# Summing the last five tiles of x in fp32 on TensorE, and turning h in one product, at the start of a two-stage attention and GEGLU kernel

## Chip, cores, metric

One core of one Trainium2 chip. The metric is the device time of one execution in microseconds; several executions of each kernel are timed. The profiled execution gives a trace and a span, from the first to the last instruction, that is some 1.7 to 2.1 us shorter than the device time.

## The reference

```python
# x: (4, 12416, 128) fp32; inducing: (32, 128); d_ff = 1536
def mab(q, kv):                                   # attention, scale = 1/sqrt(128)
    a = softmax(scale * q @ kv.T); return a @ kv
h   = mab(inducing, x)                            # 32 rows for each batch
y   = mab(x, h)                                   # one row for each token
g   = y @ w_gate
ffn = (gelu(g) * (y @ w_val)) @ w_out             # gelu with erf
out = y + sigmoid(y @ w_res) * ffn
```

The kernel folds the last four lines: `y` is `softmax * h`, so `h @ w_gate`, `h @ w_val` and `h @ w_res` are computed once for each batch (called `hgv` and `hra` below), and the softmax weights (`rt`) are multiplied with those.

## The kernel before

The first batch has a prologue of its own; after it, a long planned loop runs all gelus of all batches, with the next batch's attention in the background. The prologue has three stages. (1) Each of 13 tiles of x (97 blocks of 128 rows, 8 to a tile) is split into fp16 `hi` and `lo`, `hi` is turned on PE, scores and exps `e` follow, and `e` times (`lo` with a column of ones, `hi`) is summed in PSUM; the sum is copied out as `nacc`. (2) `finish_h` adds four strips and divides; `turn_h` turns h. (3) The second softmax, the first layer's three slices (`hgv`), the residual's product (`hra`), the load of the gelu's table, the first gelu.

```python
def accumulate(b, j0, j1, first, last):           # cut
    for j in range(j0, j1):
        o = acc[cq * M:(cq + 1) * M, :]           # one of four strips of 32 rows
        pe.matmul(o[:, 0:P + 1], e, lo_t[b, k][:, jj, :P + 1], ...)
        pe.matmul(o[:, 0:P], e, hi_t[b, k][:, jj, :], ...)
    if last: ve.tensor_copy(nacc_t[b], acc[:, :P + 1])

def first_layer(b, c):
    bank = bank_g()                               # a PSUM bank of its own
    for r, w in ((slice(0, 64), wG), (slice(64, 128), wV)):
        pe.matmul(bank[r, :], ht_t[b][:, r], w[:, c:c + TOK], start=True, stop=True)
    ve.tensor_scalar(hgv_t[b][:, c:c + TOK], bank, parts, None, op0=AL.mult)

for n in range(ntile + 2):                        # stage 1
    hi_next(n + 1)
    if n < ntile:       convert_lo(0, tiles[n], ve); turn_pe(0, tiles[n])
    if 1 <= n <= ntile: exps("a", 0, n0, n0 + w, bank_v())
    if n >= 2:          accumulate(0, n0, n0 + w, n == 2, n == ntile + 1)
for i in range(2):    weight_cast(i, act)
for i in range(2, 5): weight_cast(i, po)
finish_h(0); turn_h(0)                            # stage 2
...                                               # stage 3: exps, sums, slices
first_layer(0, 2 * TOK)
res_layer(0, ve)
gel = konst.tile([P, 1], FP32, name="gel")
act.activation(gel, parts, AC.Gelu, bias=0.0, scale=1.0)   # loads the table
warm = bank_f()
for i in range(3):
    pe.matmul(warm, wG[:, :P], wG[:, :TOK], start=True, stop=True)
```

The softmax here doesn't subtract the row's maximum and nothing guards it: scores larger than these inputs give would overflow.

## Time and profile before

| | kernel before |
|---|---|
| time, median of 3 runs (range) | 772.82 us (771.55 to 773.31) |
| span of the profiled run | 770.5 us |
| `nacc` read out of PSUM | 26.90 us |
| scores of the second softmax begin (H) | 29.10 us |
| first gelu | 35.51 us |
| from the first gelu to the end | 735.0 us |

ScalarE (ACT) runs nearly without a break from the first gelu to the end, so an edit of the prologue is worth what it moves the first gelu by. Lines from the order of time: start us, length us, engine, line, operation, out<-in; in brackets the idle time before it and what ended it.

```profile
24.35 1.83 POOL L488 CAST wG<-ge 128x1024 bf16<-128x1024 f32 x1 [22.53 <-DMA ge<-in_moe_w_gate_dram]
25.58 0.36 PE L162 MATMUL v<-I1T,xt 128*128 128x32 f16 x8 [0.48 <-ACT xt L141]
34.09 0.31 PE L249 MATMUL g<-wR,ht 128*64 128x128 bf16 x1
```

The first is a weight cast on GpSimd (POOL), the second are the scores of the last tile of x, the third is the residual's product.

### The profile page before, as it was taken

The page shows a single profiled execution, that of the slowest core. Times are in us where ns is not written, and L with a number is a line of the kernel's source. Part 1 is how long each engine was busy: PE and PEld are TensorE (multiplying, and loading weights), DVE is VectorE, ACT ScalarE, POOL GpSimd, SP SyncE. Part 2 cuts the span into 40 slices and gives each one's busy share as a digit, 9 for nine tenths or more (in the row PEclk, how much of TensorE's full clock was granted, in tenths as well). Part 3 has the DMA queues.
Part 4 walks back from the last instruction along what each step waited for, and adds up shares of the span by engine and source line. Part 5 has one row for each costly group of instructions (what it writes and reads, how often), then busy time and mean ns, then how long its engine had stood idle before and what let it go on. Part 6 is the DMA issues. An engine that isn't in the chain of part 4 may idle for free.

```text
span 770.5 us, 23888 instructions
## 1 busy us (share of the span) xinstructions
PE 738.9 (96%) x9583; PEld 432.5 (56%) x9583; DVE 741.2 (96%) x735; ACT 753.3 (98%) x1506; POOL 467.4 (61%) x470
## 2 busy tenths in 40 slices
PE   6799999999999999999999999999999999999997
PEld 4455555565655655565655555556565555555555
DVE  7699999999999999989999999998999999999997
ACT  6899999999999999999999999999999999999997
POOL 0526988822787978923377797961367773443334
PEclk9889999999999999999999999999999999999999
DMA  8314589701055677521035496750105431110101
GB/s 340 124 45 129 134 191 188 165 30 43 31 119 110 157 176 192 141 46 43 29 65 112 112 210 154 139 150 29 39 21 128 87 88 43 42 43 29 42 30 60
DMA packets 118448, 78.15 MB, mean 101 GB/s; under 512 B 96672, under 2 KB 99392, under 8 KB 118336
## 3 DMA queue, kind: packets, MB, share of 16 engines
q1 hardware_dynamic: 118336, 76.62, 39.2%
q8 instruction: 75, 1.23, 0.7%
q14 instruction: 37, 0.30, 0.1%
HBM read 27.87 MB, written 25.43 MB: 69 GB/s over the span
## 4 chain that ended last, share of the span: by engine, by line
PE 47%; ACT 35%; issue 10%; DVE 4%; POOL 3%; DMA 1%; SPq 0%; ACTq 0%; DVEq 0%; POOLq 0%
ACT ge L368 23%; PE f L391 22%; PE g L357 12%; PE v L357 7%; PE g L399 3%; DVE u L362 3%; ACT at L410 3%; ACT th L405 3%; ACT e L166 2%; ACT fe L419 2%; ACT xt L141 1%; POOL lo L124 1%; ACT L166 1%; DMA xf<-in_x_dram 1%; DMA ge<-in_x_dram 1%
## 5 line engine op out<-in xcount | busy, mean ns | idle before, releaser
L362 DVE TENSOR_TENSOR u<-ge,v 128x1024 bf16<-128x1024 f32 x584 | 671.7, 1212 | 8.2 <-PE g L357 1.9
L368 ACT ACTIVATE ge<-g 128x512 f32<-128x512 f32 x1164 | 608.3, 661 | 2.7 <-PE g L357 1.6
L391 PEld LDWEIGHTS <-u 128*128 128x128 bf16 x4656 | 270.8, 98 | 206.3 <-issue 200.4
L391 PE MATMUL f<-wO,u 128*128 128x128 bf16 x4656 | 374.4, 221 | 4.0 <-DVE th L423 0.5
L357 PE MATMUL g<-rt,hgv 32*128 32x512 f16 x1152 | 337.7, 380 | 7.3 <-ACT ge L368 0.4
L357 PE MATMUL v<-rt,hgv 32*128 32x512 f16 x1152 | 222.3, 385 | 2.5 <-DVE u L362 1.5
L424 POOL TENSOR_TENSOR at<-at,th 128x512 f32<-128x512 f32 (+1 forms) x99 | 123.6, 1248 | 147.8 <-DVE th L423 66.1
L357 PEld LDWEIGHTS <-hgv 32*128 32x128 bf16 x2400 | 75.3, 91 | 87.8 <-issue 22.8
L420 POOL TENSOR_TENSOR th<-th,fe 128x512 f32<-128x512 f32 (+1 forms) x35 | 42.2, 1205 | 92.9 <-ACT fe L419 92.9
L294 POOL TENSOR_TENSOR a<-e,z 128x1024 f16<-128x1024 f32 (+1 forms) x48 | 89.8, 1880 | 5.7 <-DMA hgv<-a 5.4
L124 POOL TENSOR_TENSOR lo<-xf,hi 128x1024 f16<-128x1024 f32 x36 | 76.8, 2135 | 0.2
L399 PE MATMUL g<-hra,rt 128*128 128x128 f16 x768 | 72.1, 219 | 1.5
L410 ACT ACTIVATE at<-g 128x512 f32<-128x512 f32 (+1 forms) x100 | 65.0, 651 | 0.0
L405 ACT ACTIVATE th<-g 128x512 f32<-128x512 f32 (+1 forms) x100 | 64.3, 650 | 0.3 <-PE g L399 0.3
L399 PEld LDWEIGHTS <-rt 128*128 128x128 f16 x768 | 50.8, 98 | 12.4 <-issue 10.4
L423 DVE SCALAR_TENSOR_TENSOR th<-th,f 128x512 f32<-128x512 f32 (+1 forms) x65 | 44.1, 678 | 3.0 <-PE f L391 0.6
L118 POOL CAST hi<-xf 128x1024 f16<-128x1024 f32 x36 | 37.4, 1038 | 11.1 <-DMA xf<-in_x_dram 6.7
L421 POOL TENSOR_TENSOR at<-at,fe 128x512 f32<-128x512 f32 (+1 forms) x35 | 42.1, 1204 | 0.0
L162 PEld LDWEIGHTS <-xt 128*128 128x128 f16 x768 | 23.4, 97 | 7.2 <-issue 3.0
L166 ACT ACTIVATE e<-g 128x512 f32<-128x512 f32 (+3 forms) x40 | 20.4, 600 | 2.4 <-PE g L162 2.2
L419 ACT ACTIVATE fe<-f 128x512 f32<-128x512 f32 (+1 forms) x35 | 22.8, 650 | 0.0
L273 POOL TENSOR_TENSOR a<-a 128x256 f32<-128x256 f32 (+8 forms) x48 | 20.0, 416 | 3.8
(113 smaller groups left out, 261.0 us busy)
## 6 DMA issues: line engine op xcount, KB each, us to landing
out_dram<-at SPq DMA_DIRECT2D x96, 256.0 KB, 2.2
xf<-in_x_dram SPq DMA_DIRECT2D x38, 512.0 KB, 4.5
ge<-in_x_dram SPq DMA_DIRECT2D x10, 512.0 KB, 8.2
rt<-a SPq DMA_TRANSPOSE x48, 3.1
xt<-hi SPq DMA_TRANSPOSE x36, 4.2
ge<-in_moe_w_gate_dram SPq DMA_DIRECT2D x1, 512.0 KB, 9.3
ge<-in_moe_w_val_dram SPq DMA_DIRECT2D x1, 512.0 KB, 9.5
ge<-in_moe_w_out_dram SPq DMA_DIRECT2D x1, 512.0 KB, 4.9
```

Source lines behind the costliest of these rows:

```text
L124: eng.tensor_tensor(lo[:, :w, :P], xf_t.pop((b, k))[:, :w, :], hi_t[b, k][:, :w, :], AL.subtract)
L166: act.activation(e[:, (j0 - t0) * M:(j1 - t0) * M], bank[:, :(j1 - j0) * M], AC.Exp, bias=0.0, scale=scale)
L294: eng.tensor_tensor(a2[:, :n], ev[:, o:o + n, :].unsqueeze(2).to_broadcast([P, n, Q, M]), z[:, o:o + n].unsqueeze(2).unsqueeze(3).to_broad ...
L357: pe.matmul(*t[n], start=True, stop=True)
L362: ve.tensor_tensor(u[:, :n], ge_t.pop(value)[:, :n], v_t.pop(value)[:, :n], AL.mult)
L368: act.activation(ge_t[i][:, h * TOK:h * TOK + n], gb[:, :n], AC.Gelu, bias=0.0, scale=1.0)
L391: pe.matmul(self.ffn[:, k, :], u_t[self.gi, si][:, o:o + P], wO[:, fc, :], start=first, stop=not self.todo, skip_group_check=True)
L399: pe.matmul(bank[:, k * P:(k + 1) * P], rt_t[self.b, self.k][:, self.j0 + k, :], hra_t[self.b][:, s, :], start=True, stop=True)
L405: act.activation(self.th[:, :self.tw], self.mix(0), AC.Tanh, bias=0.0, scale=0.5)
L410: act.activation(self.at[:, :self.tw], self.mix(1), AC.Copy, bias=0.0, scale=1.0)
L423: ve.scalar_tensor_tensor(th, th, 1.0, f, AL.add, AL.mult)
L424: (ve if self.gi == ngrp - 1 else po).tensor_tensor(at, at, th, AL.add)
```

## The change

The intent: relieve VectorE (DVE) and ScalarE in stage 1, which both are full from 15 to 25 us, by summing the five tiles that land last in fp32, as they were loaded, on PE; their exps are added up first, so that four one-column products give the denominators. Then turn and divide h in one product; load the weights behind x; and reorder stage 3, so that ScalarE's exps come first.

```diff
+            if b == 0 and k in whole:
+                pe.matmul(o[:, 0:P], e, xf_t[b, k][:, jj, :], start=False, ...)   # fp32
+                continue
+    def sum_whole(n0, w, last):          # s = sum of the exps of the fp32 tiles, on DVE
+        for s in (e_of.pop("s"), e):
+            for q in range(0, w, Q):
+                pe.matmul(acc_t[0][:, P:P + 1], s[:, q * M:(q + Q) * M], one, ...)
+    def turn_first_h(b):
+        pe.matmul(tp[:, 0:M], na[:, P:P + 1].to_broadcast([P, P]), strips[:, 0, :], ...)
+        pe.matmul(tp[:, P:2 * P], na[:, 0:P], row, ...)
+        ve.reciprocal(zi, tp[:, 0:M])
+        ve.tensor_tensor(ht, tp[:, P:2 * P], zi, AL.mult)       # cut
-            convert_lo(0, tiles[n], ve)
-            turn_pe(0, tiles[n])
+            if tiles[n] not in whole:
+                convert_lo(0, tiles[n], ve)
+            turn_pe(0, tiles[n], ve if n in (9, 11, 12) else act)
+    whole = tuple(tiles[n] for n in (8, 9, 10, 11, 12))
+    for i in range(2):                   # two empty buffers ahead of the weights
+        p_ge.tile([P, 2 * TOK], FP32, name="ge", tag="ge")
-    finish_h(0)
-    turn_h(0)
+    turn_first_h(0)
 ... exps of the second softmax ahead of the slices
-    first_layer(0, 0)
+    layers = bank_v()                                   # one tile of two PSUM banks
+    first_layer(0, 0, layers[:, :TOK])
+    first_layer(0, TOK, layers[:, TOK:])
+    finish_h(0)
+    layers = bank_v()
+    first_layer(0, 2 * TOK, layers[:, :TOK])
+    res_layer(0, ve, layers[:, TOK:])                   # the other half of the same tile
-    warm = bank_f()
-    for i in range(3):
+    warm = bank_g()
+    for i in range(2):
```

## The prediction

> **What bounds the kernel now.** I read the page's busy shares first, then the chain of waits, then the first 40 us in order of time, because the diff touches only the first batch's prologue.
>
> ```profile
> PE 738.9 (96%) x9583; PEld 432.5 (56%) x9583; DVE 741.2 (96%) x735; ACT 753.3 (98%) x1506; POOL 467.4 (61%) x470
> ```
>
> ScalarE is busy 98% of the span: from the first gelu on, the program is a loop that ACT fills. The change leaves that loop's plan as it is, so its worth is how far it moves the start of the first gelu. The timeline gives that start, and the steps on the way to it:
>
> ```profile
> 24.49 1.03 ACT L141 ACTIVATE xt<-g 128x1024 f16<-128x1024 f16 x1
> 25.98 0.38 ACT L166 ACTIVATE e<-v 128x256 f16<-128x256 f32 x1 [0.18 <-PE v L162]
> 26.90 0.29 DVE L187 COPY nacc<-f 128x129 f32<-128x129 f32 x1 [1.62 <-PE f L182]
> 27.25 0.49 PE L195 MATMUL g<-nacc,strips 128*128 128x129 f32 x2 [0.42 <-DVE nacc L187]
> 28.39 0.33 PE L214 MATMUL g<-ident,nacc 128*128 128x128 f32 x1 [0.65 <-DVE nacc L200]
> 29.10 0.55 PE L162 MATMUL g<-ht,xt 128*128 128x32 f16 x16 [0.38 <-DVE ht L216]
> 33.76 1.28 ACT L542 ACT_TABLE_LOAD   x1
> 35.09 0.38 PE L357 MATMUL g<-rt,hgv 32*128 32x512 f16 x1
> 35.51 0.60 ACT L368 ACTIVATE ge<-g 128x512 f32<-128x512 f32 x1 [0.25 <-PE g L357]
> ```
>
> Three stretches follow: up to 26.90 the sums over x; 26.90 to 29.10 (2.20 us) the turning of h; 29.10 to 35.51 (6.41 us) the second softmax's start, the folded weights and the table load. The view by windows says who bounds the first one:
>
> ```profile
> 15.00:20.00 5.00, 4.20 (x108) 3.20 (x106) 5.00 (x6) 5.00 (x10) 0.00 (x0) 1.00 1.03 410
> 20.00:25.00 5.00, 4.20 (x120) 3.25 (x118) 5.00 (x6) 5.00 (x9) 0.65 (x1) 1.00 0.79 283
> 25.00:30.00 5.00, 2.95 (x72) 1.85 (x65) 1.39 (x5) 2.77 (x7) 3.50 (x7) 1.00 0.40 116
> ```
>
> The columns after the length are PE, weight load, DVE, ACT, POOL, granted clock, DMA share, GB/s. From 15 to 25 us DVE and ACT are both full; PE has 16% left. The DMA is full to about 22 us too: the last tile of x, issued near 10.1 us, is 11.6 us under way and lands near 21.7.
>
> **What the skill says.** (1) The Trainium skill, "FP8 and Floating Point Precision", TensorE Precision Notes: a true fp32 product takes four passes. The trace agrees in kind: one fp32 product of 129 columns (L195) stands as two loads and two matmuls, some 0.11 us apart, so about 0.22 us, where an fp16 one takes 0.055. (2) "TensorEngine Tiling (Array Packing)", Available Configurations and Key Properties: 128x32 tiles give four independent column tiles, and changing the tiling mode drains the engine. The trace agrees for fp16: the last tile's 16 accumulating matmuls start at 26.41 and the engine that waits for them goes on at 26.90, where 16 in a row would need 0.9 us. No fp32 ones are packed before. (3) "VectorE: DVE Perf Modes", the perf-mode tier table: fp32 tensor_tensor runs at one element a cycle, tensor_copy up to twice that. Here `lo` takes 1.22 us and `hi` 0.69 for 1024 elements, and the fp16 copy out of PSUM 0.425 for 512. (4) "TensorE: Matmul & The Clock Gate", Part 1: a gate halves the clock after a quiet free-running window of 3.4 us. The trace shows 0.50 from about 30.9 to 34.3 and 37.7 to 44.5 us: one and two such windows.
>
> **Part 1, five tiles in fp32.** DVE loses five `lo` (5 x 1.14 = 5.7 us, start to start) and gains two `hi` (2 x 0.60), three copies out of PSUM (3 x 0.60, from 0.425 for half the size) and three sums (256 fp32 elements, 0.42, or 0.34 apart): 4.0. So DVE is relieved by 1.7 us. ACT loses two `hi` and three `xt` (5 x 0.94 = 4.7). PE pays: per tile, 16 packed fp16 matmuls (0.34) become 8 packed fp32 ones. If the four strips stay concurrent, a strip has 2 matmuls x 2 passes x 0.107 = 0.43; with loads and drain I take 0.55. New on PE are also four one-column products with `s` as weights: they pay the loads, 2 x 0.11 each, 0.88 in all, just before the last accumulation.
>
> I laid the three engines' orders (the built program gives order and waits) side by side with these durations. From the last unchanged point (14.85) DVE runs hi7, lo6, hi8, lo7, hi9 to 18.9, hi10 to 19.75, copies n9, hi11 to 20.95, then waits for the last tile (21.7). PE becomes the bound there: a round is transposes 0.49, scores 0.28, accumulation 0.55, together 1.32. Its fp32 accumulations start at 20.86, 22.19, 23.46, 24.44; the one-column products run 24.99 to 25.87; the last accumulation 25.87 to 26.42, plus 0.23 to its reader: 26.65. The same table for the kernel before gives 27.19 where 26.90 was measured, so I take off 0.29: **nacc at 26.36, 0.54 us earlier**. Each 0.15 us more per accumulation costs 0.75 in all (five tiles).
>
> **Part 2, h in one product.** Before: copy, product (0.49), reciprocal, scaling, transpose, copy, 2.20 us. After: copy 0.29; two fp32 products, 0.49 + 0.22; a reciprocal of 32 columns, 0.36 (28 took 0.33), which in the built program waits for both products; one multiply 0.29; five hand-overs of 0.05. Sum 1.84, **0.36 earlier**. Scores of the second softmax thus begin at 28.2 (H).
>
> **Part 3, from H to the first gelu.** ACT has less idle: its exps now end near H+4.0, table and `gel` near H+5.5 (6.15 before). But the order of the waits is new. PE issues, in this order: third slice of first_layer, res_layer, two warm-up matmuls, first gate. In the built program res_layer's load waits for DVE's third `hgv`, because both use halves of one PSUM tile, and the second slice waits for the first `hgv` in the same way. DVE's chain: `a` ends H+1.88, `rt` H+3.0, hgv 0.65, wait for the slice 0.46, hgv 0.65, reciprocal 0.2, hf 0.36, hgv 0.72: H+6.05. Then res_layer 0.1, two warm-ups 0.43, gate 0.38 and hand-overs: first gelu near **H+7.1 at full clock, H+8.0 at half**, against H+6.41. So ACT, done earlier, waits over a microsecond for PE, and this stretch gives back 0.7 to 1.5, say 1.0.
>
> **Part 4, weights.** The two empty tiles only swap which buffers the two pieces of w_out take: the first now waits until POOL has cast w_gate (26.2 in place of 22.4) and lands near 31. Its cast follows POOL's sums, near 33; the first use is after 37. Hidden. The other pieces are issued within 0.6 us of where they were.
>
> **Sum.** -0.54 - 0.36 + 1.0 = +0.1 us: three terms that nearly cancel. After the first gelu ACT goes on as before; it idled about 1.0 us between 39 and 45 us because of the half clock, and what falls in there can move half a microsecond either way. I go 0.5 below the sum, because the hand-overs are counted in full in part 3 and some will overlap: **772.4 us**.
>
> **Rivals.** *A: packed fp32 does not pack as well.* In-order pairs of passes on one strip could hold up the next strip: about 1.0 per accumulation, nacc at 28.4, loop 2 us later, 774.8. With no concurrency at all (8 x 0.22 + drain, 1.9) nacc is at 32.9 and the time 779. For it: no packed fp32 is in the trace. Against: the fp16 pairs before use one strip for `lo` and `hi` in the very same order, and overlapped. 20% for the first, 4% for the second. *B: the PSUM wait in part 3 does not bite*, and the loop starts when ACT is ready (H+5.9): 1.4 us gained, 771.4, or 770.5 if the clock windows help too. For it: ACT's relief is real, and the order looks meant for it. Against: the waits are in the program. 25%. *C: only the clock windows matter.* They are free-running, so the half-speed stretches fall elsewhere in each run; three runs before span 1.8 us, more than every term here. Then it is 772.8 give or take 0.9. *D: x lands late and hides everything*: the last tile at 21.7 would bound DVE; but then PE, not DVE, has the later work, so it changes little.
>
> **Range and chances.** The terms' spread is about 1 us either way, the slow fp32 adds a tail upward of 2, B one downward of 2: 770.2 to 775.0 holds 8 in 10. Faster by over 2% would need 15 us, twice what the loads and sums could free; slower by over 2% needs unpacked fp32 and more.
>
> **What would show it.** Right: the five fp32 groups about 0.55 us long each, PE over 90% busy from 20 to 26 us, nacc near 26.4; from nacc to the next scores 1.84; ACT idle of over 1 us, released by PE, before the first gelu, with PE's wait for the third hgv before it; first gelu within 1 us of 35.5; the rest of the span about 735 us in both. Wrong: accumulations of 1 us or more (A), ACT running from `gel` straight into the gelu (B), or a loop that itself changes length by more than 1 us, which none of my steps explains.

## The result

The changed kernel took 774.45 us (773.74 to 775.34, 4 runs), the kernel before in the same rounds 772.49 (771.55 to 773.31, 4 runs). The ratio is 1.0026, 95% interval 1.0009 to 1.0044. Ratios here are the mean time of one kernel's fast runs over the mean of the other's of the same rounds, so not quite the ratio of the medians quoted. By the 2% measure the time is the same, and 774.45 lies in the range predicted, but 2.0 us above the number.

In order of time, the changed kernel's lines that answer to those of before:

```profile
27.61 0.29 DVE L197 COPY nacc<-f 128x129 f32<-128x129 f32 x1 [1.75 <-PE f L187]
27.96 0.41 PE L244 MATMUL g<-strips,nacc 128*128 128x32 f32 x2 [0.42 <-DVE nacc L197]
29.45 0.59 PE L169 MATMUL g<-ht,xt 128*128 128x32 f16 x16 [0.77 <-DVE ht L250]
33.95 1.28 ACT L597 ACT_TABLE_LOAD   x1
35.17 0.74 DVE L266 TENSOR_SCALAR hgv<-v,parts 128x512 bf16<-128x512 f32 x1
35.24 0.20 ACT L597 ACTIVATE gel<-parts 128x1 f32<-128x1 f32 x1
35.97 0.32 PE L292 MATMUL v<-wR,ht 128*64 128x128 bf16 x1 [1.24 <-DVE hgv L266]
36.22 1.03 PE L600 MATMUL g<-wG 128*128 128x512 bf16 x2
37.18 0.61 PE L400 MATMUL g<-rt,hgv 32*128 32x512 f16 x2
37.87 1.57 ACT L411 ACTIVATE ge<-g 128x512 f32<-128x512 f32 x3 [2.42 <-issue]
```

`nacc` comes at 27.61 in place of 26.90: 0.71 later. From there to H (the scores at 29.45) it is 1.84 us, in place of 2.20. From H to the first gelu it is 8.42, in place of 6.41: PE stands 1.24 us before the residual's product, released by DVE's `hgv`, then runs two warm-ups and a gate at half clock, while ScalarE, ready at 35.44, idles 2.42 us ("issue" in the bracket says only that the profile found no releaser; the gate product on PE at 37.18 is what the gelu reads). From the first gelu to the end the changed kernel took 734.0 us, the kernel before 735.0.

Busy time by stretch (PE, weight load, DVE, ACT, POOL, granted clock, DMA share, GB/s):

```profile
15.00:20.00 5.00, 4.83 (x134) 3.86 (x129) 4.71 (x7) 4.58 (x9) 0.00 (x0) 1.00 1.03 402
20.00:25.00 5.00, 4.29 (x112) 3.38 (x104) 4.30 (x9) 2.42 (x5) 0.45 (x1) 1.00 0.62 238
```

ScalarE fell from 5.00 to 2.42 busy in 20 to 25 us, so the relief is real. But PE, meant to be the new bound, is busy only 4.29 of 5.00. The reason shows at the end of stage 1:

```profile
23.64 0.65 PE L187 MATMUL f<-ge,e 128*32 128x128 f32 x16
25.03 0.36 PE L169 MATMUL v<-I1T,xt 128*128 128x32 f16 x8 [0.74 <-DVE a L211]
25.33 0.65 PE L187 MATMUL f<-ge,e 128*32 128x128 f32 x16
25.92 0.60 PE L216 MATMUL f<-one,a 128*128 128x1 f32 x4
26.39 0.58 PE L216 MATMUL f<-one,e 128*128 128x1 f32 x4
26.90 0.64 PE L187 MATMUL f<-ge,e 128*32 128x128 f32 x16
```

The fp32 accumulations are as short as hoped (25.33 to 25.92, 0.59; each stands as two passes, hence x16 for 8 products). The eight records of L216 are the four one-column products: 0.98 in all. And PE stands still for 0.74 us before the last tile's scores (25.03). The profile names a DVE sum as the releaser, but the program waits there for the copy `xt`, which had ended at 24.25. What the stop cost `nacc`, and what a late sum beside it cost, is taken up under e5 and e6.

### The profile page after: what moved, and what is told of

It reads as the page before. It is cut to its first block, busy times and chain, and to the rows that moved or that the text cites. A ratio compares the mean times of both kernels' runs of the same rounds, so it can differ in the third digit from the quotient of the medians.

```text
span 771.9 us, 23907 instructions
## 1 busy us (share of the span) xinstructions
PE 741.5 (96%) x9593; PEld 434.6 (56%) x9593; DVE 740.6 (96%) x740; ACT 749.1 (97%) x1501; POOL 466.3 (60%) x465
## 3 DMA queue, kind: packets, MB, share of 16 engines
q8 instruction: 75, 1.23, 0.7%
## 4 chain that ended last, share of the span: by engine, by line
PE 46%; ACT 34%; issue 10%; DVE 5%; POOL 3%; DMA 1%; SPq 0%; ACTq 0%; DVEq 0%; POOLq 0%
ACT ge L411 23%; PE f L434 21%; PE g L400 13%; PE v L400 7%; DVE u L405 3%; PE g L442 3%; ACT th L448 3%; ACT at L453 3%; ACT e L172 2%; ACT fe L462 2%; DMA ge<-in_x_dram 1%; ACT L172 1%; PE g L169 1%; DVE lo L124 1%; POOL a L337 1%
## 5 line engine op out<-in xcount | busy, mean ns | idle before, releaser
L400 PEld LDWEIGHTS <-hgv 32*128 32x128 bf16 x2400 | 75.5, 91 | 88.5 <-issue 23.4
L169 PEld LDWEIGHTS <-xt 128*128 128x128 f16 x768 | 23.5, 97 | 6.3 <-issue 3.6
```

The lines of the kernel that those rows point to most:

```text
L400: pe.matmul(*t[n], start=True, stop=True)
```

## The experiments

My theory after the result: the loss is made in stage 3, where the residual's product waits for the third `hgv` only because both stand in halves of one PSUM tile; stage 1 adds 0.7, stage 2 takes 0.36 off. The rivals: the fp32 tiles are the whole loss; the half clock, not the wait, makes the start late; or the loop gives back whatever the start gains. All runs with 5 rounds gave correct results. Kernels ran beside the kernel before.

| run | time, median us | ratio to before [95%] | nacc to H | H to first gelu | first gelu at | rest |
|---|---|---|---|---|---|---|
| before | 772.49 | | 2.20 | 6.41 | 35.51 | 735.0 |
| changed | 774.45 | 1.0026 [1.0009, 1.0044] | 1.84 | 8.42 | 37.87 | 734.0 |
| e1 | 773.38 | 1.0013 [0.9995, 1.0031] | 2.34 | 6.30 | 36.97 | 734.2 |
| e2 | 773.80 | 1.0019 [1.0000, 1.0039] | 1.84 | 9.93 | 40.16 | 733.6 |
| e3 | 773.43 | 1.0016 [0.9999, 1.0032] | 1.83 | 8.36 | 37.64 | 735.5 |
| e4 | 773.48 | 1.0012 [0.9996, 1.0029] | 2.57 | 6.47 | 36.78 | 734.6 |
| e5 | 774.43 | 1.0029 [1.0012, 1.0045] | 2.34 | 8.29 | 38.62 | 734.3 |
| e6 | 774.24 | 1.0022 [1.0006, 1.0038] | 1.83 | 8.42 | 38.59 | 733.9 |
| e7 | 771.88 | 0.9990 [0.9972, 1.0009] | 1.83 | 5.95 | 35.29 | 735.4 |
| e8 (before) | 772.43 | 1.0001 [0.9985, 1.0018] | 2.35 | 6.57 | 35.91 | 735.4 |
| e9 | 772.37 | 0.9994 [0.9980, 1.0008] | 1.83 | 6.45 | 35.65 | 734.5 |
| e10 | 771.85 | 0.9986 [0.9972, 1.0000] | 1.83 | 5.90 | 34.78 | 734.1 |
| e11 | 773.61 | 1.0010 [0.9994, 1.0026] | 1.83 | 5.88 | 36.33 | 734.9 |
| e12 (changed) | 775.28 | 1.0031 [1.0017, 1.0045] | 2.34 | 7.72 | 37.86 | 735.1 |

The last four columns are from each run's one trace; "rest" is span less the first gelu's start. The rest is 733.6 to 735.5, the shortest of them beside the latest start (e2). A straight line through the 14 pairs has the rest fall by 0.2 us for each us of later start: the loop takes nothing more, and gives back a small part at most. A trace is of one run only: e2's was the slowest of its six (775.73), e10's the fastest of its five (770.70). Two traces of one kernel differ by half a microsecond and more in a stretch: 2.34 in place of 1.84 and 8.42 in place of 7.72 are the same instructions at half and at full clock.

**e1: the residual's product in a bank of its own.**

```diff
-    res_layer(0, ve, layers[:, TOK:])
+    res_layer(0, ve, bank_f())
```

> The changed kernel, with the residual's first product in the free one-bank PSUM buffer in place of half of the tile that the third slice of the first layer uses. Theory (the shared PSUM tile holds PE, and with it the first gelu): the 1.24 us of PE idle ahead of that product goes; product, two warm-ups and first gate then end before ScalarE has its table (35.4 us), first gelu near 35.7 in place of 37.87, and the whole time falls by about 2 us to some 772.4. Rival (the clock): the gates are slow because the clock is at half from 36 us on, gelu starts within 0.5 us of 37.9, and the time stays at 774.4. Rival (given back in the loop): gelu starts early, but the time falls by less than 0.7.

Order of time of e1:

```profile
35.57 0.40 PE L265 MATMUL v<-wV,ht 128*64 128x512 bf16 x1
35.80 0.22 PE L292 MATMUL f<-wR,ht 128*64 128x128 bf16 x1
36.50 0.20 ACT L597 ACTIVATE gel<-parts 128x1 f32<-128x1 f32 x1
36.97 4.51 ACT L411 ACTIVATE ge<-g 128x512 f32<-128x512 f32 x9 [0.26 <-POOL hra L232]
```

The product (L292) follows the slice at once, and ScalarE idles 0.26 us in place of 2.42: 6.30 from H in place of 8.42, 2.1 less. Part of that is the clock: e12 is the changed kernel with nearly e1's clock (half to 34.3 us and then full to 41.1; e1 half to 34.1 and full to 40.9), and it has 7.72, so that some 1.4 is left for the tile. The shared tile made the wait; it is 1.4 of a start that is 2.4 late. The time fell by some 1.0 us by the ratios (1.0026 to 1.0013), which lies between the theory's 2 and the rival's 0.7; the intervals are too wide to say which. The rest, 734.2, shows no giving back; this trace's `nacc` was late (28.33), with the half clock from 27.3 us on and a late sum (e5).

**e2: the wait kept, PE kept busy in it.**

```diff
+    early = bank_g()
+    for i in range(5):
+        pe.matmul(early, wG[:, :P], wG[:, :TOK], start=True, stop=True)
     res_layer(0, ve, layers[:, TOK:])
```

> The changed kernel, with five more warm-up products put ahead of the residual's first product, into a buffer of their own: PE is busy in the 1.24 us in which it idled, the wait itself stays. If the half clock after 36 us comes from that idle time and costs the start: full clock after 36, first gelu near 36.9 (about 0.9 earlier), time about 773.5. If the wait alone matters: first gelu stays within 0.3 of 37.9, and the time within 0.5 of 774.4.

By stretches in e2, cut at the clock's steps (columns as above):

```profile
29.34:32.75 3.41, 2.63 (x86) 2.45 (x83) 1.80 (x5) 1.90 (x4) 0.79 (x1) 0.51 0.08 20
32.75:36.17 3.42, 3.14 (x27) 1.42 (x25) 2.24 (x5) 2.94 (x6) 3.04 (x7) 0.50 0.00 0
36.17:39.58 3.41, 3.19 (x9) 0.84 (x8) 1.59 (x5) 0.12 (x1) 1.03 (x4) 0.50 0.00 0
```

PE busy 2.63 to 3.19 of 3.41 us did not bring the full clock back for three windows, and the five extra products, at half clock, delayed the residual's product to 38.48 and the first gelu to 40.16. Neither of the two starts expected, 36.9 and 37.9, came. The time, 773.80, is within its interval of the changed kernel's. Filling the idle time in this way is no remedy; but as the full clock never came, e2 does not show what it would have been worth. What decides the clock in these windows stays open.

**e3: everything but the fp32 tiles. e4: the fp32 tiles alone.** e3 takes `whole` back to the empty tuple, with ScalarE's conversions and copies as before; e4 puts the kernel before's whole order from `finish_h(0)` on into the changed kernel.

```diff
 e3
-    whole = tuple(tiles[n] for n in (8, 9, 10, 11, 12))
-            convert_hi(0, tiles[n], act if n in (1, 4) else ve)
+            convert_hi(0, tiles[n], act if n in (1, 4, 7, 10) else ve)
-            turn_pe(0, tiles[n], ve if n in (9, 11, 12) else act)
+            turn_pe(0, tiles[n])
 e4
-    turn_first_h(0) ... (all of the new stages 2 and 3)
+    finish_h(0); turn_h(0) ... (stages 2 and 3 of the kernel before)
```

> The changed kernel without its fp32 tiles: all tiles of x split into hi and lo as before, ScalarE converts and copies as before; the h turn, the new order of the second softmax and the weights stay. By the profile nacc came 0.71 us later with the fp32 tiles; so without them nacc is near 26.9, the scores of the second softmax start near 28.75, the first gelu near 37.2, and the time is about 773.7. Rival (the fp32 tiles are the whole loss): the time falls by 2 us or more, to 772.4 or less.

> The kernel before's order from nacc on (h turned in two steps, first layer's slices each in a bank of their own), with the five fp32 tiles and the later weights of the changed kernel ahead of it. Theory: nacc near 27.6 as in the changed kernel, then 2.20 and 6.41 us as in the kernel before: first gelu near 36.2, time about 773.2, 0.7 over the kernel before. Rival (the fp32 tiles are the whole loss): 774.4.

e3 took 773.43, e4 773.48; both ratios, 1.0016 and 1.0012, are about half of the changed kernel's. Their intervals hold 1 and 1.0026 alike, so the times alone do not divide the loss; the rival that blamed the fp32 tiles for all of it falls with e7, which keeps them and has 0.9990 [0.9972, 1.0009]. Their stretches are as foretold: e3 has the long 8.36 from H, e4 the short 6.47. e3's `nacc` was at 27.45, not the 26.9 expected: a miss, taken up under e8.

**e5: the two large weight casts on ScalarE.**

```diff
-    for i in range(2):
+    for i in range(4):
         weight_cast(i, act)
-    for i in range(2, 5):
-        weight_cast(i, po)
+    weight_cast(4, po)
```

> The changed kernel, with the two large weight casts (128x1024 fp32 to bf16) on ScalarE, which has nothing to do between the last exps over x and the second softmax, in place of GpSimd. In the traces of the changed kernel and its variants so far a DVE sum of two exps that runs while GpSimd casts takes about 1.2 us in place of 0.42. If that collision is what lengthens it: all three sums 0.42, the one-column products wait for no sum, and nacc comes 0 to 0.8 us earlier (by how the casts fell before). If the 0.6 to 0.7 us idle of PE ahead of the last tile's scores came from the collision too, it goes, and the time is some 773.4; if not, it stays, and the time is some 774.1.

In the changed kernel, and then in e5 (order of time, DVE's second and third sums, and in e5 also the last tile's scores):

```profile
24.17 1.70 DVE L211 TENSOR_TENSOR a<-a,e 128x256 f32<-128x256 f32 x2
24.55 1.04 POOL L536 CAST wG<-ge 128x1024 bf16<-128x1024 f32 x1 [22.91 <-DMA ge<-in_moe_w_gate_dram]
```

```profile
24.07 0.94 DVE L211 TENSOR_TENSOR a<-a,e 128x256 f32<-128x256 f32 x2
24.98 0.37 PE L169 MATMUL v<-I1T,xt 128*128 128x32 f16 x8 [0.79 <-DVE a L211]
```

The two sums span 0.94 us without GpSimd's casts, 1.70 with one, and 2.51 in e2's trace, where they ran beside both casts. The Trainium skill, "SBUF — State Buffer", SBUF: two separate sides, says that VectorE with two SBUF inputs and GpSimd reading SBUF share a pair of ports under an exclusive lock, and the second to start blocks fully. The traces agree: one sum of the changed kernel took 1.179 us in place of 0.415, while GpSimd's cast kept its 1.04. In the kernel before GpSimd was the loser: its cast took 1.83 beside DVE's `lo`. But PE's stop before the last tile's scores stayed (0.79), so the collision is not its cause. The one-column products that read the third sum start at 25.85 in e5 and at 25.92 in the changed kernel's trace, where that sum ended at 25.87: there the two delays lie side by side, and taking out either alone would gain less than 0.1. In e2's trace the sum ended at 26.65, and PE did wait for it, 0.78 us:

```profile
26.70 0.60 PE L216 MATMUL f<-one,a 128*128 128x1 f32 x4 [0.78 <-DVE a L211]
```

Time unchanged, 774.43.

**e6: PE's instructions shifted by 24.**

```diff
+    for i in range(12):
+        pe.matmul(i1t_ps[:, P:2 * P], identF, identF, start=True, stop=True)
     pe.transpose(i1t_ps[:, :M], ind_f, ident[:M, :M])
```

> The changed kernel, with twelve more small products (24 instructions: 12 weight loads, 12 matmuls) on PE at its very start, where it idles. In four traces with the same PE instructions up to that place PE stood still for 0.56 to 0.74 us ahead of the last tile's scores, though the copy and the products it waits for had ended. If this comes from the place in the instruction stream (a refill of instructions in blocks): the gap moves 24 instructions earlier, to the last part of the scores of the tile before or the fp32 accumulation after them, and the last tile's scores follow within 0.2 us of the accumulation. If it comes from the data or the hand-over from DVE: the gap stays where it is. Time 774.4 in both.

Order of time of e6:

```profile
19.05 0.22 PE L192 MATMUL f<-hi,e 128*32 128x128 f16 x1 [0.52 <-issue]
...
23.86 0.41 PE L187 MATMUL f<-ge,e 128*32 128x128 f32 x4
25.21 0.63 PE L187 MATMUL f<-ge,e 128*32 128x128 f32 x12 [0.93 <-issue]
25.77 0.37 PE L169 MATMUL v<-I1T,xt 128*128 128x32 f16 x8
```

The gap moved with the instructions: now it cuts the third fp32 accumulation in two, after 4 of its 16 matmul records, and the last tile's scores follow without a wait. There is a second one at 19.05. Counted over PE's records in the trace, the gaps are before the 450th and the 706th record, 256 apart; in all traces with the gap ahead of the last tile's scores these are the 706th record too. The page's DMA part says what happens there:

```profile
q8 instruction: 75, 1.23, 0.7%
```

75 packets with 1.23 MB are 16.4 KB each, and the trace's 19,201 records of PE (9,593 loads, 9,593 matmuls and 15 others) divided by 75 are 256. The Trainium skill, "Runtime: NRT & Kernel Launch", Instruction fetch mechanics, has it so: an engine's instructions are refilled in blocks of 16 KiB, 256 instructions, "mostly hidden". Here, it seems, it was not. In the changed kernel's trace that queue's second packet is under way from 22.5 to 23.5 us, 3.3 us after PE passed its 450th record (the DMA engines' share was 1.03 from 15 to 20 us and 1.05 from 22.0 to 22.5), and PE goes on at 25.03. Over six traces (changed, e1, e6, e7, e10, e12) PE goes on 1.3 to 1.5 us after that packet's end. That PE waits for this refill is inferred from the count, the shift and that steady lag; no run changed the refill alone. The refills at the boundaries near 31.4 and 49.0 us of the changed kernel's trace start within 0.4 us of them, and no stop is seen. In the kernel before the 706th record is, by chance, among the last tile's scores too, but PE came to them when ScalarE's `xt` was ready, at 25.58: the packet had ended at 23.4.

**e7: stage 3 with free banks. e8: the kernel before again.** e7 takes the casts of e5, gives the three slices three buffers (two of two banks, one of one bank), puts the residual's product in the free single bank, h's second turn after the slices, and drops the warm-ups. e8 is a copy.

```diff
-    layers = bank_v()
-    first_layer(0, 0, layers[:, :TOK])
+    first_layer(0, 0, bank_v()[:, :TOK])
-    first_layer(0, TOK, layers[:, TOK:])
+    first_layer(0, TOK, bank_v()[:, :TOK])
-    finish_h(0)
-    layers = bank_v()
-    first_layer(0, 2 * TOK, layers[:, :TOK])
-    res_layer(0, ve, layers[:, TOK:])
+    first_layer(0, 2 * TOK, bank_g())
     ones_b(0, half, WIDE)
     weights_b(0, 0, half, PRE)
+    finish_h(0)
+    res_layer(0, ve, bank_f())
-    warm = bank_g() ... (two products)
```

> The changed kernel with its PSUM waits taken out of the start: the first layer's three slices in three different buffers, the residual's product in the free one-bank buffer, h for the residual after the slices, the weights of the second softmax's rest ahead of it, no warm-ups, and the large casts on ScalarE. Theory (the first gelu's start sets the time, and PE's waits set that start): ScalarE goes from its table straight into the first gelu, idle under 0.15 us in place of 2.42; from the scores of the second softmax to the first gelu 6.0 us in place of 8.42; time 2 to 2.5 us under the changed kernel, some 772.2. Rival (given back later): the start comes early, but the time stays above 773.2.

> The kernel before, unchanged, for a second trace: how far the landing of the last tile, nacc (26.90 us) and the first gelu (35.51 us) move between two traces of the same kernel. If they move by less than 0.3 us, the differences between the traces are the kernels'; if by 0.7 or more, only stretches within a trace can be compared. Time 772.5.

Order of time of e7:

```profile
29.34 0.57 PE L169 MATMUL g<-ht,xt 128*128 128x32 f16 x16 [0.77 <-DVE ht L250]
35.18 0.20 ACT L594 ACTIVATE gel<-parts 128x1 f32<-128x1 f32 x1
35.29 3.59 ACT L411 ACTIVATE ge<-g 128x512 f32<-128x512 f32 x7
```

ScalarE goes from its table into the first gelu without a gap; 5.95 from H. The time is 771.88 against 774.43 and 774.24 of e5 and e6 on the same chip: 2.4 to 2.6 us less, where the two do what the changed kernel does in stage 3. The clock's windows lie within half a microsecond of the changed kernel's (half from 29.6 to 33.0 and from 36.4 us), so the 2.5 us less from H are not theirs. The theory holds for stage 3 as a whole: its new order and waits made the late start, and with them gone the loss is gone; e7 takes several out at once, so it gives no share to any one. e8 moved by 0.09 in `nacc` (26.99) and 0.40 in the first gelu (35.91), the latter with the half clock from 27.7 us on. So some 0.4 us of the first gelu can be noise of the clock, but that does not explain e3's `nacc`: e3 (27.45) and e9 (27.37), both without fp32 tiles, are 0.4 to 0.5 us later than both traces of the kernel before (26.90, 26.99). In these two ScalarE's first `hi`, which waits for x, began at 6.53 and 6.47, in all other traces at 6.16 to 6.34. Whether that is chance or comes of the code stays open; by these traces not all of the 0.71 is the fp32 tiles'.

**e9: e7 without the fp32 tiles. e10: one one-column product in place of four. e11: e10 with PE's instructions shifted. e12: the changed kernel again.**

```diff
 e10, on e7
-        for s in (e_of.pop("s"), e):
-            for q in range(0, w, Q): pe.matmul(acc_t[0][:, P:P + 1], s[...], one, ...)
+        folded = []                               # halves added on DVE
+        for s in (e_of.pop("s"), e):
+            ve.tensor_tensor(t, s[:, :Q * M], s[:, Q * M:], AL.add); folded.append(t)
+        ve.tensor_tensor(folded[0], folded[0], folded[1], AL.add)
 in accumulate, after the last tile's products
+            pe.matmul(acc[:, P:P + 1], e_of.pop("fold"), one, start=False, stop=True, ...)
 e11, on e10
+    for i in range(82):
+        pe.matmul(i1t_ps[:, P:2 * P], identF, identF, start=True, stop=True)
```

> The kernel with the PSUM waits taken out of the start (free banks, large casts on ScalarE), and without the fp32 tiles: hi and lo as in the kernel before. If the fp32 tiles cost some 0.5 us as written: nacc near 27.0, scores of the second softmax 1.84 later, first gelu 6.0 after that, near 34.9, time about 771.4 (the same kernel with fp32 tiles: 771.9). If the fp32 tiles gain as predicted once the start is free: 772.4.

> The kernel with free banks and fp32 tiles, the four one-column products ahead of the last accumulation (0.98 us of PE) folded into one after it: VectorE, idle there, adds the two halves of the sum, the two of the last exps, and both. PE gains three products, and the last accumulation no longer stands behind them: nacc about 0.7 us earlier than with the four (27.5 to about 26.8), time 771.2. If PE's stop ahead of the last tile's scores or the landing of x hides it, nacc moves by under 0.3, and the time stays at 771.9.

> The kernel of the folded sum, with 82 small products (164 PE instructions) more at the very start. The stops of PE came at its 450th and 706th records, 256 apart, whatever these were. If that holds: no stop ahead of the last tile's scores; one instead at the start of the second fp32 accumulation (its 706th record now), and the 962nd falls on the wait for ht, where it costs nothing. nacc then 0 to 0.4 us earlier, since the moved stop still stands on PE's full stretch; time 771.0 to 771.4. If the stop belongs to the last tile: it stays there.

> The changed kernel once more, beside the three above and for a second trace. Time 774.4; PE idle 1.24 us ahead of the residual's product and ScalarE over 2.2 us ahead of the first gelu, as in its first trace; the stop ahead of the last tile's scores 0.5 to 0.8 us; nacc between 27.6 and 28.4.

e9 took 772.37 (0.9994), e7 771.88 (0.9990): with stage 3 free, the fp32 tiles neither gain nor lose anything that the intervals could show. The traces put `nacc` at 27.37 without them and 27.51 with them.

e10 took 771.85 beside 772.97 for the kernel before and 775.28 for the changed one (e12) on the same chip. Order of time of e10:

```profile
25.01 0.36 PE L169 MATMUL v<-I1T,xt 128*128 128x32 f16 x8 [1.01 <-DVE a L214]
25.30 1.19 PE L187 MATMUL f<-ge,e 128*32 128x128 f32 x32
27.05 0.29 DVE L200 COPY nacc<-f 128x129 f32<-128x129 f32 x1 [0.47 <-PE f L196]
34.78 1.06 ACT L417 ACTIVATE ge<-g 128x512 f32<-128x512 f32 x2
```

The last two accumulations (x32) now follow each other, and `nacc` is at 27.05, 0.46 before e7's in place of the 0.7 expected; PE's stop, 1.01 us in this trace, is still in it. The first gelu, 34.78, is the earliest of all. Its ratio, 0.9986 [0.9972, 1.0000], is the lowest of all, 1.1 us under the kernel before, with the interval just touching 1: not clear of noise.

e11 was a miss in its cost. Order of time of e11:

```profile
1.78 6.18 PE L517 MATMUL g<-identF 128*128 128x128 f16 x82 [1.78 <-DVE strips L510]
...
25.52 0.65 PE L187 MATMUL f<-ge,e 128*32 128x128 f32 x16
26.18 0.36 PE L169 MATMUL v<-I1T,xt 128*128 128x32 f16 x8
```

The 82 products took 6.18 us in all, 0.075 each, so that the first tile was turned at 9.02 in place of e10's 5.57, and everything after came later; this trace also has a half-clock window from 11.7 to 15.1 us, which the others do not. The time was 773.61. But the last tile's scores follow the accumulation with no stop, as the place in the stream foretold. The stop that I expected at the new 706th record is not there either: its packet was over at 21.2, and PE came there only near 22.8, 1.6 us later, when by the lag of the other traces the block was ready.

e12 repeats the changed kernel: 775.28, 1.0031. Order of time:

```profile
25.18 0.36 PE L169 MATMUL v<-I1T,xt 128*128 128x32 f16 x8 [1.17 <-DVE a L211]
36.68 0.24 PE L292 MATMUL v<-wR,ht 128*64 128x128 bf16 x1 [1.24 <-DVE hgv L266]
37.86 4.52 ACT L411 ACTIVATE ge<-g 128x512 f32<-128x512 f32 x9 [1.66 <-POOL hra L234]
```

The 1.24 us of PE ahead of the residual's product are there again to the hundredth. The clock was full from 34.3 to 41.1 us this time, so warm-ups and gate were quick, and ScalarE idled 1.66 in place of the "over 2.2" that I expected; the stop of PE was 1.17, longer than the 0.5 to 0.8 expected.

## Why the prediction was right or wrong

The time, 774.45, fell in the range of 770.2 to 775.0, near its upper end, and the class was right. That owes more to the width of the range than to the sum. The number, 772.4, was 2.0 us low; of the prediction's own signs of being right three failed (PE over 90% busy from 20 to 26 us: 88%; `nacc` near 26.4: 27.61; first gelu within 1 us of 35.5: 37.87), and the others held. Two of its terms and one choice were mis-sized:

- **Part 1, nacc 0.54 us earlier: wrong, it came 0.71 later.** The fp32 accumulations fit (0.57 to 0.59 for 0.55 taken), and rival A falls with them; that its 774.8 is near the measured time is chance. The table of starts had the four at 20.86, 22.19, 23.46, 24.44; they were at 21.01, 22.33, 23.64 and 25.33. The first three are 0.14 to 0.18 late; the fourth is where the step failed: PE stopped for 0.74 us, by all signs at an instruction refill (e6, e11), of which I had no term. Nor had I one for the third sum, which took 1.18 us beside GpSimd's cast, not 0.42, and ended only at 25.87: without the stop it would have held the one-column products just as long in this trace. In e5 and e7, without the collision, the stop alone still held them to 25.85 and 25.82. The one-column products cost 0.98, not 0.88. And the 0.29 that I took off because the same table was late for the kernel before was not to be had here. 0.15 + 0.74 + 0.10 + 0.29 is 1.28, the miss 1.25. That e3 and e9 are late too, without fp32 tiles, is not explained by these terms.
- **Part 2, 1.84 in place of 2.20: right**, to the hundredth at full clock, which is luck in the last digit: the terms listed add up to 1.90, and the hand-overs, taken as 0.25, measured 0.18. At half clock it is 2.34 (e1, e5, e12), where the kernel before's order has 2.35 (e8) and 2.57 (e4).
- **Part 3, the mechanism right, the size wrong.** The wait of the residual's product on the third `hgv` is there, as is the chain behind it (1.24 us of PE in both traces, gone in e1 and e7). I gave H+7.1 at full and H+8.0 at half clock, and measured 7.72 (e12) and 8.42. The third `hgv` ended at H+6.46, not H+6.05; the exps and slices ahead of it ran partly at half clock. From there to the gelu I had 1.95 at half clock, and it was 1.96. Then I took +1.0 for the stretch, between the 0.7 and 1.6 that H+7.1 and H+8.0 give, nearer to the full clock's; four of the five traces that have this stage 3 unaltered (changed, e3, e5, e6, against e12) had the half clock from 36 to 37 us on. The term was +2.0. ScalarE's own chain was too short as well: `gel` ended at H+5.99, not H+5.5, where the kernel before has 6.16. So even with PE's waits gone there was little to gain in this stretch: e7 has 5.95, against 6.41 and 6.57 in the kernel before.
- **Part 4, weights hidden: right.** No step of the start waited for a weight in either trace; the casts did delay a sum on DVE (part 1).
- **The half microsecond taken off the sum** for hand-overs that would overlap was a choice against the evidence; the table of part 3 was already too short.
- Measured, the terms are +0.71 - 0.36 + 2.01 = +2.36 for the first gelu in the first trace; the span grew by 1.4 and the median time by 2.0. That the loop keeps its length (733.6 to 735.5 in 14 traces) was right.
- **Rival B** (the wait does not bite) was false for the changed kernel; e7, which also drops the warm-ups and moves casts, shows about what it would have been: 771.9, where I had said 771.4 or 770.5. **Rival C** (only the clock) falls: the changed kernel's two intervals exclude 1, and e7 differs from e5 and e6 by some 2.4 us or more; the windows do move single traces by half a microsecond. **Rival D**: the last tile's `hi` waited 0.59 us for its load and set nothing, as said.

What is not settled: the share of each part in the time. e3 and e4 put some 0.9 to 1.2 us on each half of the change, e7 and e9 nothing on the fp32 tiles; the intervals are 1.1 to 1.5 us to either side. Nor is it shown what made `nacc` late in e3 and e9, or what a version without PE's stop would reach, since e11 paid for its shift elsewhere.

## What to carry to other kernels

When an edit relieves two engines and loads a third, follow it to the next hand-over: here ScalarE's relief of several microseconds ended in a late start, the largest part shown of it a wait made by two products that shared one PSUM tile without sharing data. Look in the built program for waits between halves of a tile, and give late, unrelated products buffers of their own. Where an engine goes from waiting to being the bound, costs that its waits had covered can appear: here, it seems, the refill of its own instructions. And where two delays end together, taking out one shows nothing: try both.

## What the Trainium skill lacked or had wrong

- "Runtime: NRT & Kernel Launch", Instruction fetch mechanics: blocks of 256 instructions are borne out (gaps ahead of PE's 450th and 706th record; 75 packets for 19,201 records), and an fp32 product counts as four (two loads, two matmuls). "Mostly hidden" did not hold here while the DMA engines were full or had just been: PE stood 0.52 to 1.17 us at a boundary, the packet started 3.1 to 3.9 us after the boundary before it and PE went on 1.3 to 1.5 us after it ended. The page has no such times, nor how to see it: the profile names another engine, or "issue", as the releaser.
- "TensorE: Matmul & The Clock Gate", Part 1: it gives the clock as full after one busy window or more. In e2 PE was busy 2.63 and 3.14 of 3.41 us in two windows, and the clock stayed at 0.50 through the next; in e9 it stayed there for four windows, 13.65 us, in the second of which the profile has PE busy for all 3.41. The page does not say what counts as busy.
- "TensorEngine Tiling (Array Packing)": it has no figure for fp32 products in 128x32 tiles. Eight of them with 128 columns took 0.57 to 0.59 us start to start, four one-column fp32 products with full 128x128 weights 0.98.
- "SBUF — State Buffer", SBUF: two separate sides: nothing found wrong; the sum took 1.179 us in place of 0.415 as the second to start.
